# Weights of k and v in a ring of six tiles, those of q in a ring of two, 64 bytes apart

## The chip, the cores and the metric

The kernel runs on one core of one Trainium2 chip. The metric is the device time of one execution in microseconds (us). Where a time comes from the profile, it is from one profiled execution; times inside it count from the start of its span.

## What is computed

A block of attention with a compressive memory, followed by an MLP that mixes tokens, both behind layer norms whose scale and shift come from a condition vector. There are 2048 tokens of 1024 channels, 32 heads of 32, and 4 segments of 512 tokens.

```python
def _A_ref(x, wq, wk, wv, wo, beta):
    q, k, v = (heads of x @ wq, x @ wk, x @ wv)     # 32 heads, 4 segments of 512
    for s in range(4):
        logits = qs @ ks.T * scale + mask           # key <= query is kept
        a_dot = softmax(logits) @ vs
        a_mem = (phi(qs) @ M) / (phi(qs) @ z + 1e-6)
        outs.append(g * a_mem + (1 - g) * a_dot)
        M, z = M + phi(ks).T @ vs, z + sum(phi(ks))
    return o @ wo

x = x + ga * _A_ref(layernorm(x) * (1 + ca) + sa, ...)
h = layernorm(x) * (1 + cb) + sb
x = x + gb * _B_ref(h, ...)     # U = (W2 gelu(W1 LayerNorm(h)^T))^T, F = 3584
```

`sa, ca, ga, sb, cb, gb` are the six parts of `silu(c) @ w_mod`.

## The kernel before

**Stages.** The first stage projects q, k and v and runs the attention; the output projection (`out_proj`) follows, and then the two matrix products of the token MLP (`mix`, line 798), done with seven products in place of eight. Every matrix product of fp32 values is made of three passes: each operand is split into a high part and a low part (`split`, lines 120 and 123: a cast on ACT, a subtraction on DVE), and high times high, high times low and low times high are added up.

**The first stage.** The heads are taken in 8 groups of 4. The work goes in two passes `pr`: the first takes segments 0 and 1 of all groups, the second segments 2 and 3. A pass over one group and one segment is a task `t`, 32 in all: tasks 0 to 15 are the first pass, 16 to 31 the second, and two tasks that follow each other share a group and so its weights. The normalized input of a segment lies in eight "h pages" of 4096 bytes per partition.

A task is projected in four pieces (`project`). Pieces 0 and 1 make k and v, 48 matmuls each (`kv_chunk`, line 193, `nps<-wv,h`: the h page is the stationary operand, the weights stream); piece 2 transposes k (line 363) and makes q, 24 matmuls (`q_chunk`, line 201, `qps<-h,wq`: the weights are stationary, the h page streams). After that, twelve DMAs (`stack`, lines 325 to 327, `sk<-sg`) bring queries and keys of the four heads into the tiles `sk`.

For each head, `maxima` (line 431) computes the scores once for the row maxima. Every second head, the maxima are transposed (line 438, `nmps`), split by ACT and DVE into `nt`, and four small DMAs (line 445, `sk<-nt`) write them into rows 96 and 97 of `sk`. `scores` (lines 466 to 473, `a<-sk`) then computes the scores again with the maxima subtracted; it has to wait for these DMAs. ACT takes the exponential, POOL masks, and `values` (line 495) multiplies by v.

**The weights.** A group has six weight tiles of 4096 bytes per partition: four for k and v together (`wv`, two parts of two tiles) and two for q (`wq`). In the first pass they come as fp32 from the input (`fetch_part`), are split on the chip (`split_part`), and are written to the DRAM tensor `wsp` (`keep_w`, line 174). In the second pass they are read back from `wsp` already split, by one DMA per tile (`load_part`, line 168). All tiles come from one pool, `paw`, with one tag and eight buffers: a ring. A new tile has to wait until the last matmul that reads the buffer's former tile is over. In the order of the tiles (v, v, v, v, q, q for each group) a tile takes the buffer of the tile eight places before it.

**What sets the order.** A scheduler with a timeline of its own orders the instructions of each engine, within the data dependencies and within the places in the program at which the kernel calls for each step. A tile of a ring can be placed only when its buffer is free on that timeline. All DMAs are issued from SP, in one queue: also the condition's rows (`rawm`), the output weights (`wor`), the h pages of the second pass (`h<-hT`, line 310), and the results (`oT`).

**Addresses.** Pools opened one after the other lie one behind the other in SBUF. Behind `paw` come the tiles of the projections (`prj`), of the values (`late`) and `sk`. Some pools begin with a small tile that is used for nothing but its size (`pad`, `pad2`, `offset`, each 32 bytes per partition). In this kernel the h pages lie at 1760 + 4096 n, the weight tiles at 97952 + 4096 n.

Of the kernel before, what the change touches and what calls it, by code (L numbers as in the profile page):

```python
# [7 lines left out]
F32 = mybir.dt.float32  # L8
F32R = mybir.dt.float32r
# [9 lines left out]
P = 128  # L19
# [25 lines left out]
def attention_and_mlp(ctx, tc, x, wq, wkv, wo, beta, w1, b1, w2, b2, c, wm_a, wm_b, out):  # L45
# [70 lines left out]
    def split(dst, src, hi_eng, lo_eng):  # L116

        hi, lo = dst[:, 0], dst[:, 1]
        if hi_eng is A:
            A.copy(hi, src)  # L120
        else:
            hi_eng.tensor_copy(hi, src)
        lo_eng.tensor_tensor(lo, src, hi.bitcast(F32), op=ALU.subtract)  # L123
# [20 lines left out]

    paw = tc.tile_pool(name="paw", bufs=1)
    aw = paw.__enter__()
    raw_w = {}

    def fetch_part(g, kind, part):
        r = a.tile([P, D], F32, tag="raw", bufs=3, name=f"raw{kind}{g}_{part}")  # L150
        SY.dma_start(r, (wkv if kind == "v" else wq)[g, :, 1024 * part:1024 * part + 1024])
        return r

    def split_part(g, kind, part, r):

        for i in range(2):
            w = aw.tile([P, 2, 512], F32R, tag="w", bufs=8, name=f"w{kind}0_{g}_{part}_{i}")
            split(w, r[:, 512 * i:512 * i + 512], A, V)
            W[0, g][kind, 2 * part + i] = w

    def load_part(g, pr, kind, part, res):

        if pr == 0:
            split_part(g, kind, part, fetch_part(g, kind, part))
            return
        for i in range(2):
            w = aw.tile([P, 2, 512], F32R, tag="w", bufs=8, name=f"w{kind}{pr}_{g}_{part}_{i}")
            SY.dma_start(w.bitcast(F32), wsp[g, 2 * part + i if kind == "v" else 4 + i])
            res[kind, 2 * part + i] = w

# [5 lines left out]
    def load_w(g, pr):  # L176
        res = W[pr, g] = {}
        for kind, part in (("v", 0), ("v", 1), ("q", 0)):
            load_part(g, pr, kind, part, res)
        if pr == 0:  # L180
            keep_w(g)
# [92 lines left out]
    for ct in range(NK):  # L274
        for part in range(2):
            wm = s1p.tile([P, D], F32, tag="wm", bufs=11, name=f"wm{ct}_{part}")
            last_wm = SY.dma_start(wm, wm_a[part, ct])
            if part == 0:
                V.scalar_tensor_tensor(wm, wm, 1.0, scb, op0=ALU.mult, op1=ALU.mult, accum_out=saca[:, ct, 0:1])
            else:  # L280
                for k in range(NK):
                    T.matmul(scale_ps[:, ct:ct + 1], wm[:, P * k:P * k + P], sc[:, k:k + 1], start=(k == 0),
                             stop=(k == NK - 1), skip_group_check=True)
        if ct < 3:
            load_part(0, 0, *(("v", 0), ("q", 0), ("v", 1))[ct], W[0, 0])
        V.tensor_scalar_add(saca[:, ct, 1:2], scale_ps[:, ct:ct + 1], 1.0)
        h_chunk(s1p, xs[0], 0, ct)
        if ct:
            first_chunk(ct - 1)
    first_chunk(NK - 1)  # L290
    left.__exit__(None, None, None)
    prj = tc.tile_pool(name="prj", bufs=1, reuse_waits="tile")
    pj = prj.__enter__()
    late = tc.tile_pool(name="late", bufs=1, reuse_waits="tile")
    b = late.__enter__()
    skp = [tc.tile_pool(name=f"sk{i}", bufs=1, reuse_waits="tile") for i in range(2)]
# [309 lines left out]
    for g in range(2, NG):  # L606
        n = 8 * g - 13
        plan(n, lambda g=g: W.__setitem__((0, g), {}))
        for kind, part, n0, n1 in (("v", 0, 0, 1), ("v", 1, 1, 3), ("q", 0, 2, 4)):
            later(n + n0, lambda g=g, kind=kind, part=part: fetch_part(g, kind, part),  # L610
                  n + n1, lambda r, g=g, kind=kind, part=part: split_part(g, kind, part, r), "A")
        plan(n + 4, lambda g=g: keep_w(g))
    for j in range(32):
        n = ML0 + MLS * j
        later(n, lambda j=j: mod_fetch(j), n + 2, lambda r, j=j: mod_late(j, r), "V")
    plan(WO0 - 3, lambda: spread(gaw, 0))
    for i in range(8):
        n = WO0 + WOS * i
        later(n, lambda i=i: wo_fetch(i), n + 2, lambda r, i=i: wo_split(i, r), "G")

    for n in range(-LEADS, 4 * NI + VL):
# [15 lines left out]
        if 4 * NI - 5 <= m < 4 * NI + 3:  # L637
            i = m - 4 * NI + 5
# [4 lines left out]
            with behind(n, engines):  # L643
                f()
    right.__exit__(None, None, None)
    for q in skp + [late, prj, paw]:
        q.__exit__(None, None, None)


# [6 lines left out]
    w = cw_pool.__enter__()  # L656
# [344 lines left out]
```

## Time and profile before

| | us |
|---|---|
| median of 3 runs | 2305.62 |
| lowest and highest | 2304.03, 2310.8 |
| the profiled execution | 2305.58 |
| its span | 2303.9 |

The engines are PE (TensorE matmul), PEld (its weight loads, which overlap PE), DVE (VectorE), ACT (ScalarE), POOL (GpSimd) and SP (SyncE, which here only issues DMAs; SPq is its queue). A name like `qps<-h,wq` is the tile written and the tiles read, L201 a line of the kernel. Matmuls are pipelined: one takes about 0.39 us from its start to its end, and the next starts before that, so the pace of a row of matmuls is the distance of their starts. The clock is the share of its full clock that TensorE was granted.

### The profile page before, as it was taken

The numbers are of one execution on the slowest core, as the hardware profiler recorded it, in microseconds if no ns is written. First come the engines' busy times: TensorE is split into PE (matmuls) and PEld (weight loads), VectorE is DVE, ScalarE is ACT, GpSimd is POOL, SyncE is SP. The second block draws the span as 40 slices with busy tenths as digits, with TensorE's granted clock in tenths as the row PEclk, the third lists the DMA queues.
The fourth block names the chain that finished last, engine by engine and source line by source line (L and its number), as shares of the span: only waits on it lengthen the run. The fifth ranks groups of instructions, "written<-read, shape, count | busy, mean of one in ns | idle before, by whom it ended". The sixth has DMA issues, their size and how long they took to land.

```text
span 2303.9 us, 38456 instructions
## 1 busy us (share of the span) xinstructions
PE 2232.7 (97%) x13866; PEld 1918.9 (83%) x13866; DVE 1703.9 (74%) x3814; ACT 1105.6 (48%) x2018; POOL 727.9 (32%) x835
## 2 busy tenths in 40 slices
PE   8989999998999999999999999999999999999999
PEld 7879888898998889977787888888887888888877
DVE  5666666775777777657988665688889787878787
ACT  5477766755656656654324333543334242424232
POOL 3165655655666767653001000023333000000000
PEclk9989999999999999989999999999999999999999
DMA  6656555677566566663466664556557441414133
GB/s 256 199 164 183 173 162 162 195 247 225 156 199 206 166 189 187 202 212 112 137 205 213 249 237 181 202 222 239 206 201 263 171 151 55 151 55 142 55 119 146
DMA packets 172593, 414.67 MB, mean 180 GB/s; under 512 B 17236, under 2 KB 71540, under 8 KB 163444
## 3 DMA queue, kind: packets, MB, share of 16 engines
q1 hardware_dynamic: 172404, 412.22, 54.7%
q8 instruction: 110, 1.80, 0.3%
q14 instruction: 79, 0.65, 0.1%
HBM read 236.23 MB, written 125.06 MB: 157 GB/s over the span
## 4 chain that ended last, share of the span: by engine, by line
PE 81%; DVE 9%; DMA 5%; ACT 2%; issue 1%; POOL 1%; SPq 0%; DVEq 0%; ACTq 0%
PE mx L798 41%; PE nps L193 14%; PE qps L201 7%; PE po L706 6%; PE pv L495 3%; DMA wr<-in_w_dram 1%; PE a L466 1%; PE sx L431 1%; DVE ac L805 1%; PE sz L431 1%; DVE bU L123 1%; PE rd L403 1%; DVE sp L123 1%; DMA sk<-nt 1%; PE a L469 1%
## 5 line engine op out<-in xcount | busy, mean ns | idle before, releaser
L798 PE MATMUL mx<-bU,sp 128*128 128x512 f32 x2352 | 537.0, 390 | 4.7 <-DVE ac L805 2.0
L798 PEld LDWEIGHTS mx<-bU,sp 128*128 128x128 f32 x2352 | 440.4, 188 | 100.8 <-DVE sp L123 2.7
L193 PE MATMUL nps<-wv,h 128*128 128x256 f32 x3072 | 438.2, 284 | 0.7 <-DVE sg L123 0.5
L798 PE MATMUL mx<-bA,sp 128*128 128x512 f32 x1764 | 432.0, 390 | 2.5 <-DVE sp L123 2.2
L120 ACT CAST sp<-wr 128x384 fp32r<-128x384 f32 (+2 forms) x408 | 217.1, 545 | 449.9 <-PE mx L798 379.6
L481 POOL TENSOR_TENSOR ph<-p,ph 128x640 f16<-128x640 f32 x256 | 379.6, 1504 | 159.0 <-ACT ph L479 153.5
L193 PEld LDWEIGHTS nps<-wv,h 128*128 128x128 f32 x3072 | 403.8, 190 | 6.8 <-DVE sg L123 0.7
L798 PEld LDWEIGHTS mx<-bA,sp 128*128 128x128 f32 x1764 | 330.5, 188 | 73.5 <-DVE sp L123 2.9
L123 DVE TENSOR_TENSOR sp<-wr,sp 128x384 fp32r<-128x384 f32 (+2 forms) x408 | 256.8, 641 | 29.4 <-ACT sp L120 29.2
L805 DVE TENSOR_TENSOR ac<-mx,ac 128x512 f32<-128x512 f32 x280 | 189.3, 685 | 91.2 <-PE mx L798 90.5
L201 PE MATMUL qps<-h,wq 128*128 128x512 f32 x768 | 200.7, 406 | 1.4 <-DVE r L356 1.4
L432 DVE CUSTOM_DVE_ANT_0 sx<-sx,mask 128x128 f32<-128x128 f32 (+1 forms) x256 | 109.5, 428 | 113.6 <-PE sx L431 111.9
L706 PE MATMUL po<-wo,ots 128*128 128x512 f32 x768 | 184.8, 400 | 5.3 <-DVE x L709 3.1
L479 ACT CAST ph<-p 128x1280 f16<-128x1280 f32 x128 | 160.8, 1257 | 41.1 <-POOL p L477 40.3
L706 PEld LDWEIGHTS po<-wo,ots 128*128 128x128 f32 x768 | 148.3, 194 | 38.0 <-issue 3.9
L201 PEld LDWEIGHTS qps<-h,wq 128*128 128x128 f32 x768 | 144.4, 194 | 30.2 <-DVE r L356 1.2
L798 PE MATMUL mx<-bB,sp 128*128 128x512 f32 x588 | 164.3, 389 | 0.0
L477 POOL TENSOR_SCALAR_AFFINE_SELECT p<-p 128x256 f32<-128x256 f32 x256 | 120.5, 480 | 129.2 <-ACT p L470 63.4
L495 PE MATMUL pv<-vp,ph 128*128 128x97 bf16 (+1 forms) x2560 | 146.6, 204 | 5.5 <-DVE mv L134 2.7
L495 PEld LDWEIGHTS <-ph 128*128 128x128 f16 x2560 | 117.5, 100 | 29.4 <-issue 12.1
L805 DVE TENSOR_TENSOR cc<-mx,cc 128x512 f32<-128x512 f32 x140 | 94.6, 683 | 49.9 <-PE mx L798 45.4
L798 PEld LDWEIGHTS mx<-bB,sp 128*128 128x128 f32 x588 | 110.4, 188 | 23.4 <-ACT bB L120 0.6
(173 smaller groups left out, 3206.0 us busy)
## 6 DMA issues: line engine op xcount, KB each, us to landing
sk<-sg SPq DMA_DIRECT2D x384, 128.0 KB
wr<-in_w_dram SPq DMA_DIRECT2D x28, 1024.0 KB
wr<-in_w_dram SPq DMA_DIRECT2D x32, 768.0 KB
bstu<-ucd SPq DMA_DIRECT2D x28, 768.0 KB
wsp<-wv SPq DMA_DIRECT2D x32, 512.0 KB
rawm<-in_wm_b_dram SPq DMA_DIRECT2D x32, 512.0 KB
wv<-wsp SPq DMA_DIRECT2D x32, 512.0 KB
pcd<-cc SPq DMA_DIRECT2D x14, 1024.0 KB
```

The source lines that it names most:

```text
L120: A.copy(hi, src)
L123: lo_eng.tensor_tensor(lo, src, hi.bitcast(F32), op=ALU.subtract)
L193: T.matmul(ps[:, aa], h[:, j, 128 * tt:128 * tt + 128], wt[:, i, o:o + 256], start=(n == 0), stop=(n >= 6 * NK - 2), skip_group_check=True)
L201: T.matmul(ps, wt[:, i, o:o + 128], h[:, j], start=(k + n == 0), stop=(3 * k + n == 3 * NK - 1))
L432: marks[4 * t + h - LEADS, "V"] = V.tensor_tensor_reduce(o, o, mask[:, 384 - 128 * i:], 1.0, -3.0e38, op0=ALU.add, op1=ALU.max, accum_out= ...
L477: G.affine_select(w, w, pattern=[[0, 2], [1, 128]], compare_op=ALU.is_ge, fill=0.0, base=0, channel_multiplier=-1)
L479: marks[n, "A"] = A.copy(ph[:, 0], p32)
L481: marks[n, "G"] = G.tensor_tensor(ph[:, 1, c], p32[:, c], ph[:, 0, c], op=ALU.subtract)
L495: T.matmul(pv[:, i, 0:w], ph[:, part, o:o + 128], d["vp"][:, j, h, 0:w], start=(n == 0), stop=(n == 19), skip_group_check=True)
L706: T.matmul(ps, os_[:, i, P * ct:P * ct + P], wop[ct, nh][:, j], start=(n == 0), stop=(n == 3 * NK - 1))
L798: T.matmul(ps, ops[q][:, i, P * k:P * k + P], b[:, j], start=(m == 0 and first), stop=(m == 3 * nk - 1), skip_group_check=True)
L805: V.tensor_tensor(d, ps, d, op=ALU.add)
```

## The change

The one ring of eight tiles becomes two: six buffers for the tiles of k and v in the pool `paw`, and two buffers for the tiles of q in a pool of their own, `paq`, opened behind it. The new pool begins with an unused tile of 64 bytes per partition, `pad3`, so the q tiles start 64 bytes behind the end of the others, and every pool that is opened later on this side during the first stage lies 64 bytes further on. The number of weight tiles, eight, is the same.

```diff
     paw = tc.tile_pool(name="paw", bufs=1)
     aw = paw.__enter__()
+    paq = tc.tile_pool(name="paq", bufs=1)
+    awq = paq.__enter__()
+    awq.tile([P, 16], F32, name="pad3")
+
+    def weight_tile(kind, name):
+        pool, n = (aw, 6) if kind == "v" else (awq, 2)
+        return pool.tile([P, 2, 512], F32R, tag="w" + kind, bufs=n, name=name)
+
     raw_w = {}
...
     def split_part(g, kind, part, r):
 
         for i in range(2):
-            w = aw.tile([P, 2, 512], F32R, tag="w", bufs=8, name=f"w{kind}0_{g}_{part}_{i}")
+            w = weight_tile(kind, f"w{kind}0_{g}_{part}_{i}")
             split(w, r[:, 512 * i:512 * i + 512], A, V)
             W[0, g][kind, 2 * part + i] = w
...
             split_part(g, kind, part, fetch_part(g, kind, part))
             return
         for i in range(2):
-            w = aw.tile([P, 2, 512], F32R, tag="w", bufs=8, name=f"w{kind}{pr}_{g}_{part}_{i}")
+            w = weight_tile(kind, f"w{kind}{pr}_{g}_{part}_{i}")
             SY.dma_start(w.bitcast(F32), wsp[g, 2 * part + i if kind == "v" else 4 + i])
             res[kind, 2 * part + i] = w
...
-    for q in skp + [late, prj, paw]:
+    for q in skp + [late, prj, paq, paw]:
         q.__exit__(None, None, None)
```

## The prediction

> **What bounds the kernel now.** I read the page's busy shares and its chain first, then stretches of time, then who waited for whom.
>
> ```profile
> PE 2232.7 (97%) x13866; PEld 1918.9 (83%) x13866; DVE 1703.9 (74%) x3814; ACT 1105.6 (48%) x2018; POOL 727.9 (32%) x835
> PE 81%; DVE 9%; DMA 5%; ACT 2%; issue 1%; POOL 1%; SPq 0%; DVEq 0%; ACTq 0%
> ...
> 0.00:485.00 485.00, 452.40 (x3710) 410.33 (x3711) 325.67 (x950) 320.39 (x604) 256.42 (x328) 0.96 0.62 187
> 485.00:1040.00 555.00, 536.23 (x4635) 486.46 (x4633) 381.35 (x1182) 335.50 (x595) 356.33 (x430) 0.97 0.66 199
> 1040.00:2303.90 1263.90, 1244.05 (x5528) 1022.09 (x5526) 996.85 (x1684) 449.73 (x820) 115.15 (x79) 1.00 0.48 169
> ```
>
> TensorE bounds it: 97% busy, 81% of the chain that ended last. The three lower lines are stretches of time (length, then busy time of PE, PEld, DVE, ACT, POOL, then granted clock, DMA share, GB/s). The weights that change place are used in the first two; TensorE is idle there for 485 - 452.4 = 32.6 us and 555 - 536.2 = 18.8 us. A change of buffers can give back only such idle time, the loss of clock that goes with it, or matmul pace. Who does TensorE wait for?
>
> ```profile
> PE a L466 <- DMA sk<-nt: 8.2, 4, 2.8
> PE kps L363 <- DVE r L356: 8.2, 5, 4.1
> PE nps L193 <- ACT wv L120: 0.2, 1, 0.2
> ```
>
> These are total us, times, longest, over the whole run. For weights TensorE waits once, 0.2 us; no line names wq. The ring of eight costs TensorE nothing now, so freeing its tiles earlier cannot pay by itself.
>
> **The change, part by part.**
>
> *Waits on the rings.* With one ring of eight and six tiles per group, the first two v tiles of a group take over the q tiles of two groups before, the other v tiles the first v tiles of the group before, and the q tiles its last v tiles. With six and two, the later v tiles wait for the same tiles as now, the first two v tiles may come earlier, and each q tile waits for the q tile of the group just before, so it is released by a q matmul, not by the last kv matmul. One group boundary of the second pass, tasks 17 to 18:
>
> ```profile
> 582.07 0.64 PE L193 MATMUL nps<-wv,h 128*128 128x256 f32 x4
> 584.61 4.36 PE L201 MATMUL qps<-h,wq 128*128 128x512 f32 x18
> 590.83 0.63 PE L201 MATMUL qps<-h,wq 128*128 128x512 f32 x2
> 613.06 3.62 PE L201 MATMUL qps<-h,wq 128*128 128x512 f32 x15
> 616.98 1.78 PE L201 MATMUL qps<-h,wq 128*128 128x512 f32 x7
> ```
>
> Now the loads may start when the last kv matmul is over, at 582.7. After the change the second one must wait for the last q matmul, at 591.5, which leaves 613.1 - 591.5 = 21.6 us to the next q matmul. Each load is 0.524 MB; at the stretch's 199 GB/s that is 2.6 us (my estimate), 5.3 us for both. The wait is covered four times over. In the first pass ACT and DVE write the tiles:
>
> ```profile
> L120 ACT CAST wq<-rawq x16: 603/623/648, 18.9 to 475.4; 128x512 fp32r<-128x512 f32 x16
> L123 DVE TENSOR_TENSOR wq<-rawq,wq x16: 680/1494/1904, 19.5 to 477.3; 128x512 fp32r<-128x512 f32 x16
> ```
>
> Two tiles cost 2 x (0.62 + 1.49) = 4.2 us there, in a gap of the same kind. Queued behind a waiting split are ACT's copies of scores and projections; behind a waiting load, SP's transfers of keys, queries and maxima. If the cover went, each of the seven group boundaries of a pass would cost TensorE up to the load, some 5 us. Taken: 0, bounds 0 and 2 us.
>
> *Order.* The scheduler frees tiles at other moments, so it orders some instructions anew. In the built program each engine holds the same instructions. The order is the same up to the end of task 12's scores and task 14's queries, that is to about 485 us, and again after task 31's last transposes; between, 1,644 of 16,170 TensorE entries stand elsewhere, 340 of DVE's 3,774, 176 of ACT's 2,018, 110 of SP's 1,238 and 75 of POOL's 838. So the first stretch cannot gain from order, nor the third. In the second, TensorE alternates between kinds of matmul 2,213 times instead of 2,207; the 18-row above gives a bound for one alternation (pace below): (4.36 - 0.39) - 17 x 0.2267 = 0.12 us. Six make +0.7 us.
>
> *Placement.* In the built program the q tiles start 64 bytes further on (122,592 against 118,432 + 4,096) and so do the pools after them. Modulo 2,048 bytes a q tile then lies as the h pages do; now it lies 64 bytes off. Operands that lie alike, and q as it is:
>
> ```profile
> L193 PE MATMUL nps<-wv,h 128*128 128x256 f32 x3072 | 438.2, 284 | 0.7 <-DVE sg L123 0.5 <-ACT wv L120 0.2
> 1498.61 1.98 PE L798 MATMUL mx<-bA,sp 128*128 128x512 f32 x8
> 1500.42 0.84 PE L798 MATMUL mx<-bB,sp 128*128 128x512 f32 x3
> L798 PE MATMUL mx<-bB,sp 128*128 128x512 f32 x588 | 164.3, 389 | 0.0
> L201 PE MATMUL qps<-h,wq 128*128 128x512 f32 x768 | 200.7, 406 | 1.4 <-DVE r L356 1.4
> ```
>
> Take one matmul's 0.39 us from a row and divide by the rest: mx with bB (alike modulo 2,048) goes at (0.84 - 0.39)/2 = 0.225 us, with bA (256 bytes off) at (1.98 - 0.39)/7 = 0.227 us; q, in the boundary's last two rows, at (3.62 - 0.39)/14 = 0.2307 to (1.78 - 0.39)/6 = 0.2317 us. (A kv matmul, in that boundary's first row: (0.64 - 0.28)/3 = 0.12 us.) So lying alike does no harm, and q is 4 to 5 ns over the best pace: 768 x 4.5 ns = 3.5 us at most, if it is the place and not the neighbours of q in this stage. Bounds 0 and -3.5; I take -1.5, nearer to nothing, since bA is as fast without lying alike. The Trainium skill (TensorE: Matmul & The Clock Gate, what happens when you issue a matmul, LDWEIGHTS step) gives TensorE two independent read ports, one for the moving operand and one for weights, so placement would matter nothing. By that rule this term is 0.
>
> *Stalls.* The rest is which short transfers come late in the second stretch.
>
> ```profile
> 523.32 0.56 PE L466 MATMUL a<-sk 98*128 98x512 f32 x1 [1.85 <-DMA sk<-nt]
> 544.69 0.50 PE L466 MATMUL a<-sk 98*128 98x512 f32 x1 [1.32 <-DMA sk<-nt]
> 556.39 0.47 PE L466 MATMUL a<-sk 98*128 98x512 f32 x1 [1.81 <-ACT p L474]
> 702.54 0.47 PE L466 MATMUL a<-sk 98*128 98x512 f32 x1 [2.21 <-DMA sk<-nt]
> 786.41 0.77 PE L466 MATMUL a<-sk 98*128 98x512 f32 x1 [2.83 <-DMA sk<-nt]
> ...
> 523.60:527.00 3.40, 3.40 (x15) 3.12 (x14) 1.50 (x6) 1.75 (x3) 1.59 (x3) 0.50 0.96 349
> 557.70:564.50 6.80, 6.10 (x28) 5.34 (x28) 4.35 (x14) 3.52 (x6) 5.43 (x5) 0.50 0.38 122
> 786.40:789.80 3.40, 3.39 (x26) 2.91 (x27) 0.59 (x2) 2.52 (x4) 0.61 (x1) 0.50 0.00 0
> ```
>
> Three of these are followed by a stretch at half clock, 3.4 or 6.8 us long, which costs half its length again: 1.7 or 3.4 us. The Trainium skill (same page, HAM oscillation) says to avoid TensorE gaps over about 3.4 us; these rows show half clock after gaps of 1.8 to 2.8 us, so the rows disagree with that limit. By it a new 2 us stall would cost its 2 us alone.
>
> The stall at 702.5 (task 19, heads 2 and 3) comes from this queue:
>
> ```profile
> 691.09 1.60 SPq L168 DMA_DIRECT2D wv<-wsp  x1
> 692.73 0.43 SPq L520 DMA_DIRECT2D rawm<-in_wm_b_dram  x1
> 693.21 0.44 SPq L578 DMA_DIRECT2D wor<-in_wo_dram  x1
> 693.75 0.41 SPq L520 DMA_DIRECT2D rawm<-in_wm_b_dram  x1
> 694.26 0.38 SPq L168 DMA_DIRECT2D wv<-wsp  x1
> 694.73 0.39 SPq L168 DMA_DIRECT2D wq<-wsp  x1
> 696.93 2.64 SPq L445 DMA_DIRECT2D sk<-nt  x4
> ```
>
> Six large loads go ahead of the four small ones, and only 39 matmuls stand between the transpose of the maxima and the waiting score matmul. After the change task 19 has 65 there, 24 of them of q (24 x 0.23 = 5.5 us): that stall goes. Task 25 comes to exactly the old case, 39 matmuls of the same kinds instead of 62 and six large loads ahead: +2.2. In task 22 it is 31 instead of 42 (13 kv matmuls fewer, bounded by 13 x 0.12): +1.5 on 2.83. In tasks 13 and 14 TensorE has less between as well (116 to 75, 159 to 119), but two v loads leave the crowd ahead of those transfers. Sum: -2.2 + 2.2 + 1.5 = +1.5, with one or two half-clock stretches either way, -5 to +5.
>
> **Sum.** 0 + 0.7 - 1.5 + 1.5 = +0.7 us on the profiled execution's 2305.58 (span 2303.9 and 1.7 around it), which lies 0.04 under the median of 2305.62: **2306.3 us**. With the bounds of the terms (-9 to +9) the forecast's own range is 2297 to 2315.
>
> **Rivals.** *Slower: the small transfers of tasks 13 and 14 stay where they are and TensorE arrives earlier.* Against 523.3, 41 matmuls fewer stand ahead, 22 of them of q: 22 x 0.231 = 5.1 us more stall. Against 544.7 there are 40 fewer, 23 of kv (23 x 0.12 = 2.8). With a half-clock stretch more for each (2 x 1.7): +11.3 on the forecast, 2317.6. For it: 96% DMA share and 349 GB/s in the row of 523.6, a full queue. Against: the first two v loads of the second pass go out before task 12's transfers and take 1 MB, about 3 us at that rate, out of the crowd. It decides if those small transfers land less than some 4 us earlier after task 13's queries than now.
>
> *Faster: the emptier queue removes the stalls at 523, 545 and 556* and their half clock: 1.85 + 1.32 + 1.81 + 1.7 + 3.4 = 10.1, that is 2296.2. For it: the same two loads. Against: TensorE's orders above take away as much slack as the queue gains.
>
> *Placement is worth more, or less, than the q rows show.* All 3.5 us give 2304; sk and the projections' tiles move by 64 bytes too, and no row prices that. It stays within the range.
>
> *The change does nothing:* 2305.6, if order and queue drift cancel; it falls within the forecast's class.
>
> **Numbers.** 0.3% is 6.9 us, about what a measurement of this kernel can tell from no change. Forecast and the two cases near it, within 6.9 us: 0.50. The slower rival, or the forecast's own upper end: 0.30. The faster one, or its lower end: 0.20. To leave out no more than 2 in 10 the range must reach past both rivals: 2294 to 2321. The likeliest case's own range is 2297 to 2315.
>
> **What would show it.** Right: the q loads in the second pass go out after the last q matmul of the group before, and no wait names wq; the first 485 us keep their length to 2 us; q's pace falls to about 0.227 us; the stall at task 19 is gone and one at task 25 is there. Wrong: a wait of TensorE for wq, by which the cover was not there; kv or q pace worse by over 5 ns, by which placement costs; stalls at L466 in tasks 13 to 15 that add to over 10 us, the slower rival; or a change in the third stretch, where only addresses before it differ.

## The result, and the profile after

| | before | after |
|---|---|---|
| median, us | 2306.98 (10 runs on the same chip) | 2313.77 (10 runs) |
| lowest and highest | 2303.33, 2310.8 | 2305.68, 2319.48 |
| ratio to before, 95% interval | | 1.003 (1.0016 to 1.0043) |
| the profiled execution | 2305.58 | 2319.48 (span 2317.8) |

The change costs 6.8 us, 0.3%. The profiled execution of after is the slowest of its ten, 5.7 us over the median; that of before lies 1.4 us under its median. So no length of after below is read alone: the same order of instructions was profiled twice more, in `rings_no_gap` and `rings_again` below, at 2305.98 and 2308.0 us, each the fastest execution of its kernel. The order of before was profiled twice more as well, in `one_ring_gap` and `one_ring_shifted`.

The busy line of after's page, then the prediction's three stretches (length, busy PE, PEld, DVE, ACT, POOL, granted clock, DMA share, GB/s):

```profile
PE 2237.2 (97%) x13866; PEld 1923.5 (83%) x13866; DVE 1701.2 (73%) x3814; ACT 1107.6 (48%) x2018; POOL 722.1 (31%) x835
```

```profile
0.00:485.00 485.00, 452.00 (x3680) 410.96 (x3681) 324.84 (x938) 319.00 (x601) 254.11 (x324) 0.96 0.60 186
485.00:1040.00 555.00, 532.34 (x4621) 482.16 (x4619) 371.85 (x1181) 334.25 (x590) 346.59 (x425) 0.98 0.63 194
1040.00:2303.90 1263.90, 1244.17 (x5531) 1023.87 (x5532) 999.39 (x1690) 454.38 (x828) 121.39 (x88) 0.99 0.48 170
```

TensorE still bounds the kernel. Its busy time in the first and third stretch is as before (452.40 and 1244.05); in the second it fell from 536.23 to 532.34, which is 3.9 us more idle time in 555 us. Stretches at fixed times hold different work, so the next view cuts at marks of the program: the first q matmul of tasks 14, 16, 18, 24 and 31, and the first matmul of the output projection of the ninth of its 16 token tiles. Before, then after:

```profile
487.60:549.21 61.61, 58.16 (x488) 52.42 (x488) 37.02 (x117) 30.89 (x58) 28.79 (x37) 0.97 0.88 300
549.21:613.06 63.85, 61.30 (x538) 56.07 (x537) 41.93 (x132) 37.91 (x68) 38.50 (x45) 0.95 0.60 167
613.06:790.28 177.22, 171.38 (x1526) 157.47 (x1526) 128.66 (x389) 110.42 (x198) 122.21 (x144) 0.99 0.64 188
790.28:991.59 201.31, 198.55 (x1787) 182.94 (x1786) 140.45 (x442) 128.02 (x227) 135.45 (x167) 1.00 0.61 178
991.59:1057.04 65.45, 57.66 (x404) 46.70 (x403) 42.35 (x122) 36.26 (x60) 42.21 (x50) 0.86 0.60 198
sum 569.44, PE 547.05 PEld 495.60 DVE 390.40 ACT 343.49 POOL 367.17; mean PE 109.41 PEld 99.12 DVE 78.08 ACT 68.70 POOL 73.43
```

```profile
490.83:554.85 64.02, 59.80 (x514) 54.16 (x513) 37.79 (x123) 34.68 (x63) 31.77 (x42) 0.95 0.89 289
554.85:612.20 57.35, 57.21 (x527) 52.73 (x525) 38.82 (x127) 36.08 (x66) 35.18 (x43) 1.00 0.57 167
612.20:792.35 180.15, 171.37 (x1506) 156.37 (x1504) 126.72 (x385) 109.65 (x196) 116.87 (x142) 0.99 0.62 185
792.35:1002.07 209.72, 204.59 (x1809) 187.39 (x1809) 140.45 (x445) 130.27 (x229) 138.15 (x168) 0.98 0.57 171
1002.07:1069.44 67.37, 56.51 (x387) 44.37 (x384) 43.88 (x125) 34.97 (x58) 39.65 (x49) 0.89 0.60 200
sum 578.61, PE 549.48 PEld 495.03 DVE 387.67 ACT 345.65 POOL 361.62; mean PE 109.90 PEld 99.01 DVE 77.53 ACT 69.13 POOL 72.32
```

In both the five rows hold 4,743 matmuls, though some have crossed from one row to the next. Tasks 14 to 18 take 4.1 us less than before (121.37 against 125.46), all later rows 13.3 us more. TensorE's idle time over the five is 569.44 - 547.05 = 22.4 us before, 578.61 - 549.48 = 29.1 us after.

Who it waits for there (total, times, longest, from 485 to 1070 us), before and after:

```profile
PE a L466 <- DMA sk<-nt: 8.2, 4, 2.8
PE pv L495 <- DVE mv L134: 2.7, 1, 2.7
PE sz L431 <- DVE mx L432: 2.5, 2, 2.3
PE a L466 <- ACT p L474: 1.8, 1, 1.8
```

```profile
PE a L474 <- DMA sk<-nt: 9.2, 6, 4.0
PE pv L503 <- DVE red L510: 3.7, 4, 2.1
PE sx L439 <- DVE mx L440: 2.9, 2, 2.7
PE po L714 <- DMA wo<-wos: 2.2, 1, 2.2
PE po L714 <- ACT ots L120: 1.7, 1, 1.7
PE pv L503 <- POOL v L348: 1.5, 1, 1.5
```

The small transfers `sk<-nt`, the only waits that the prediction counted, rose by 1.0 us in this execution. That is no more than scatter: they come to 6.8 to 9.6 us in the three profiles of before's order and to 7.1 to 9.2 us in the three of after's. The others are waits for vector results, copies and output weights: the three others of before went or shrank to 0.6 us or less, and the five others of after were not there before or were shorter. Four of these five come back in both other profiles of after's order; the one for `mx` does not (0.8 and 0.4 us there). The three that before never shows at this size, in `rings_no_gap`:

```profile
PE po L713 <- DMA wo<-wos: 3.8, 1, 3.8
PE pv L502 <- DVE red L509: 3.7, 4, 2.1
PE pv L502 <- POOL v L347: 1.5, 1, 1.5
```

No wait names wq.

### The profile page after: what moved, and what is told of

Read it like the earlier page. It is cut to its first block, busy times and chain, and to the rows that moved or that the text cites. A ratio compares the mean times of both kernels' runs of the same rounds, so it can differ in the third digit from the quotient of the medians.

```text
span 2317.8 us, 38439 instructions
## 1 busy us (share of the span) xinstructions
PE 2237.2 (97%) x13866; PEld 1923.5 (83%) x13866; DVE 1701.2 (73%) x3814; ACT 1107.6 (48%) x2018; POOL 722.1 (31%) x835
## 4 chain that ended last, share of the span: by engine, by line
PE 75%; DMA 10%; DVE 9%; ACT 2%; issue 2%; POOL 1%; SPq 1%; DVEq 0%; ACTq 0%; POOLq 0%
PE mx L806 37%; PE nps L201 12%; PE qps L209 8%; PE po L714 5%; PE pv L503 3%; DMA xb<-x1d 2%; DMA x1e<-xb 2%; DMA sk<-nt 1%; PE a L474 1%; PE sx L439 1%; DVE bU L123 1%; PE sz L439 1%; DMA x<-in_x_dram 1%; PE rd L411 1%; PE a L477 1%
## 5 line engine op out<-in xcount | busy, mean ns | idle before, releaser
L489 POOL TENSOR_TENSOR ph<-p,ph 128x640 f16<-128x640 f32 x256 | 374.1, 1482 | 156.1 <-ACT ph L487 150.3
L209 PE MATMUL qps<-h,wq 128*128 128x512 f32 x768 | 205.5, 414 | 1.5 <-DVE r L364 1.5
L209 PEld LDWEIGHTS qps<-h,wq 128*128 128x128 f32 x768 | 149.7, 201 | 31.6 <-issue 1.6
L503 PEld LDWEIGHTS <-ph 128*128 128x128 f16 x2560 | 116.7, 100 | 31.4 <-issue 11.4
```

Source lines behind the costliest of these rows:

```text
L209: T.matmul(ps, wt[:, i, o:o + 128], h[:, j], start=(k + n == 0), stop=(3 * k + n == 3 * NK - 1))
L489: marks[n, "G"] = G.tensor_tensor(ph[:, 1, c], p32[:, c], ph[:, 0, c], op=ALU.subtract)
L503: T.matmul(pv[:, i, 0:w], ph[:, part, o:o + 128], d["vp"][:, j, h, 0:w], start=(n == 0), stop=(n == 19), skip_group_check=True)
```

## The experiments

In each table the ratio is to runs of the kernel before on the same chip.

**Is it the order or the place?** The change does two things after 485 us: it re-sorts instructions, and it moves tiles by 64 bytes. Four kernels separate them. `rings_no_gap` keeps the two rings, and so after's order on every engine, but drops the gap, so that the q tiles and the later pools lie as before:

```diff
     awq = paq.__enter__()
-    awq.tile([P, 16], F32, name="pad3")
```

> The two rings without the 64 bytes between them: every engine's order of instructions is that of the changed kernel, every tile but q's lies where it lay before, and q is again 64 bytes off the h pages (modulo 2,048). If the new order from about 485 us on costs the 6.8 us: 2312 to 2317, that is 5 to 10 above the kernel before, with the stalls at the score matmuls of tasks 13 and 25 there. If the placement costs it: within 3 us of the kernel before. The pace of a row of q matmuls should go back from 0.227 to about 0.230 us, which is worth 2 us.

`one_ring_gap` is the kernel before, in its order, with only the unused 64 bytes behind the one ring, so that the later pools lie as after:

```diff
     aw = paw.__enter__()
+    paq = tc.tile_pool(name="paq", bufs=1)
+    awq = paq.__enter__()
+    awq.tile([P, 16], F32, name="pad3")
```

> One ring of eight as before, with 64 unused bytes behind it: every engine's order is that of the kernel before, the weight tiles lie where they lay, and all pools behind them (projections, values, sk) lie 64 bytes further on, as in the changed kernel. If order costs the 6.8 us: within 3 us of the kernel before, 2304 to 2310. If the shift of those pools costs it: 2311 to 2316. q stays at 0.230 us.

`one_ring_shifted` puts the 64 bytes ahead of the ring, so that all eight weight tiles lie as the h pages do modulo 2,048 bytes; the order is that of before:

```diff
     aw = paw.__enter__()
+    aw.tile([P, 16], F32, name="pad3")
```

> One ring of eight as before, but all eight tiles 64 bytes further on, and the pools behind them too: the order of the kernel before, and both q and the kv weights now lie as the h pages do modulo 2,048. If lying alike is what brings q to 0.227 us, q goes to 0.227 here too (2 us gained) and the kv matmuls go from a mean of 119.7 ns to some 117 or less (up to 6 us gained): 2299 to 2305. If the pace of q came from something else in the changed kernel: no change of pace, 2304 to 2310. If kv is worse when alike: slower, over 2310.

`rings_again` is after unedited. It ran late, beside the last experiment below.

> The changed kernel once more, unedited, on the same chip as the kernel with the earlier load, so that the two stand against the same runs of the kernel before. Both theories: 1.002 to 1.0045, TensorE idle 28 to 30 us from task 14's queries to po8_0, and the wait for wo<-wos of 2 to 4 us there again.

| kernel | order | median us | ratio, 95% interval | five rows: length, PE busy, idle |
|---|---|---|---|---|
| before | before | | | 569.4, 547.1, 22.4 |
| one_ring_gap | before | 2306.29 | 1.0001 (0.999 to 1.0013) | 569.2, 546.5, 22.7 |
| one_ring_shifted | before | 2306.16 | 1.0005 (0.9993 to 1.0016) | 571.0, 549.8, 21.2 |
| after | after | 2313.77 | 1.003 (1.0016 to 1.0043) | 578.6, 549.5, 29.1 |
| rings_no_gap | after | 2312.49 | 1.0033 (1.002 to 1.0046) | 574.7, 546.3, 28.5 |
| rings_again | after | 2316.54 | 1.0037 (1.0019 to 1.0055) | 574.8, 548.2, 26.6 |

All kernels in the order of before are within 0.16% of it, wherever the tiles lie; all in the order of after lose 0.3%, with the gap or without. The cost is that of two rings and the order that comes with them. The idle time parts the kernels the same way: 21 to 23 us against 27 to 29. Row by row, over three profiles each:

| TensorE idle, us | order of before | order of after |
|---|---|---|
| tasks 14 to 16 | 3.5 to 4.0 | 3.7 to 4.2 |
| tasks 16 to 18 | 1.5 to 3.2 | 0.1 |
| tasks 18 to 24 | 4.2 to 5.8 | 6.6 to 8.8 |
| tasks 24 to 31 | 2.5 to 3.1 | 4.4 to 5.1 |
| task 31 to the output projection | 7.3 to 8.8 | 10.9 to 13.1 |

So the new order gains in the second row and loses in the last three, most of all in the last.

Of the expectations, that of `one_ring_shifted` missed: q became faster as it says, but the kv matmuls became slower and the time stayed where it was (see the last section). For `rings_again`, 28 to 30 us idle and a wait of 2 to 4 us for wo were expected, and 26.6 and 1.4 came.

**How much of it is clock?** Most runs are on record with the mean clock that TensorE was granted. It averages 0.983 in each of three sets of runs of before and in `one_ring_gap`, and 0.982, 0.9825 and 0.981 in after, `rings_no_gap` and `rings_again`. Time multiplied by clock is an estimate of the time at full clock: 2267 us in the three sets of before and in `one_ring_gap`, 2271 to 2273 us in the three of after's order. By it 4 to 5.5 us of the loss would be there at full clock too, and the other 2 to 5 us go with the lower clock. No run parts the two: where the prediction shows stretches at half clock, they follow waits of TensorE, so the lower clock can itself come from longer waits.

**Do the early v loads crowd the queue?** In `rings_v_behind_q` the first two v loads of each group in the second pass stay behind the q loads of the group before, as the one ring had them (the lines that note the last load are left out here):

```diff
...
-            load_part(g, pr, kind, part, res)
+            with ExitStack() as s:
+                if pr and (kind, part) == ("v", 0):
+                    s.enter_context(tc.issue_after(last_load["q"].ins))
+                load_part(g, pr, kind, part, res)
```

> The two rings and the 64 bytes, but in the second pass the loads of a group's first two v tiles are queued on SP behind the loads of q of the group before, as the one ring forced them to be; q's tiles still wait for the q matmuls of the group before. TensorE's order is a third one. If early v loads crowding the queue ahead of the small transfers of the maxima are what costs the time: 2304 to 2309, with the waits for those transfers back to some 8 us or less. If any new order costs something by the stalls it happens to hold: anywhere from 2304 to 2318, and no less waiting than in the changed kernel (some 11 us for the small transfers).

Measured: 2313.22 us, 1.0033 (1.0017 to 1.0048), idle 29.8 us, 9.8 us of it for the small transfers. Task 13's wait, the first line, is short, but others are long:

```profile
526.33 0.47 PE L478 MATMUL a<-sk 98*128 98x512 f32 x1 [1.17 <-DMA sk<-nt]
788.83 0.77 PE L478 MATMUL a<-sk 98*128 98x512 f32 x1 [3.66 <-DMA sk<-nt]
1024.74 0.80 PE L443 MATMUL sz<-sk 96*128 96x512 f32 x1 [3.35 <-DVE mx L444]
```

The edit sorted TensorE's instructions into a third order, neither before's nor after's. So it shows that late v loads alone do not give the time back, not what they cost by themselves.

**Do the weight loads ahead of the small transfers cost it?** In `rings_nt_first` and `one_ring_nt_first` a group's loads in the second pass are issued behind the small transfers of the maxima just traced, with two rings and with one (the lines that note the last small transfer are left out):

```diff
...
-                with tc.issue_after(last_sk[0, 3].ins):
+                with tc.issue_after((last_nt[0] if its[t][0] else last_sk[0, 3]).ins):
                     load_w(its[t][1], its[t][0])
```

> The changed kernel, with the loads of a second-pass group's weights queued on SP behind the small transfers of the maxima of heads 2 and 3 of the task two before the group's first. Those transfers then have no weight load right ahead of them, and TensorE's order is sorted anew. If the changed kernel lost its 7 us by weight loads ahead of the small transfers: 2304 to 2308, with TensorE's waits for them at no more than 5 us (10.9 in the changed kernel), the one of task 13 (4.0 and 3.7 us in two executions of that order) under 2. If the loss is spread over whatever waits a new order holds: still 2308 to 2317, the wait of task 13 smaller and others in its place.

> The same queueing with the one ring of eight of the kernel before. If the small transfers are what costs: faster than the kernel before by the part of its 8.2 us and their half clock that goes, 2297 to 2303. If a new order mostly trades waits: 2304 to 2316.

Measured: 2320.65 us, 1.0062 (1.0045 to 1.008), idle 35.0, and 2312.04 us, 1.0028 (1.0014 to 1.0043), idle 28.9. Task 13's wait is down to 0.5 us with two rings, but the waits for small transfers still come to 7.2 us, and to 9.5 us with one ring. So moving the loads does not remove these waits. With two rings these stand out, the second of them for a weight tile:

```profile
785.59 0.77 PE L475 MATMUL a<-sk 98*128 98x512 f32 x1 [3.97 <-DMA sk<-nt]
827.07 1.12 PE L201 MATMUL nps<-wv,h 128*128 128x256 f32 x6 [1.65 <-DMA wv<-wsp]
973.28 0.63 PE L519 MATMUL ops<-ident,am 128*128 128x128 f32 x4 [3.61 <-POOL p L486]
```

**Are two q buffers too few?** `rings_4_4` gives four to each kind:

```diff
-        pool, n = (aw, 6) if kind == "v" else (awq, 2)
+        pool, n = (aw, 4) if kind == "v" else (awq, 4)
```

> Two rings of four, 64 bytes apart: eight tiles as ever, but now q's tiles are free a whole group early, and the first v tiles wait for the first v tiles of the group before. If it is the late release of q's tiles that costs: 2304 to 2308. If any new order costs: 2308 to 2318; a price of the v tiles' later release would show as a wait of the kv matmuls for wv. q should run at 0.227 us in rows.

Measured: 2323.34 us, 1.0072 (1.005 to 1.0094), idle 30.9. Task 13's wait is as long as after's:

```profile
525.05 0.77 PE L474 MATMUL a<-sk 98*128 98x512 f32 x1 [4.21 <-DMA sk<-nt]
```

No wait of TensorE names wv or wq. Spare q buffers do not help; whether v's ring of four costs by itself was not separated.

**What does any new order cost?** `mx3` leaves the weights as before and gives a small tile of maxima a third buffer, an edit that has nothing to do with the rings:

```diff
-            d["mx"] = b.tile([P, 2, 4], F32, tag="mx", bufs=2, name=f"mx{t}_{h}")
+            d["mx"] = b.tile([P, 2, 4], F32, tag="mx", bufs=3, name=f"mx{t}_{h}")
```

> One ring of eight as before, and one change that has nothing to do with weights: the tile of the row maxima has three buffers of 32 bytes instead of two. No instruction is added and one constraint is loosened; the scheduler sorts the order anew (4,932 of 16,170 TensorE entries elsewhere, more than by the rings). If the order of the kernel before is simply a good one of many, this one costs as well: 2308 to 2320. If only orders with late q loads cost: 2302 to 2308.

Measured: 2310.07 us, 1.0011 (0.9997 to 1.0024), idle 21.9; 4,932 of TensorE's entries moved. Unclear, at most 0.24%. So a new order can be nearly free, but of the six orders tried none beat that of before, and five are slower by 0.28 to 0.72%.

**Is a single wait behind it?** At the end of the stage the eighth load of output weights stands behind all twelve `sk<-sg` transfers of task 31 in after, where before all eight went in a row. `rings_wo_first` moves it ahead of the first nine, and leaves every other instruction of every engine at its place:

```diff
-            for h in range(3):
+            for h in range(3 if t < NI - 1 else 0):
                 stack(t, h)
...
+            if m == 4 * NI - 2:
+                with tc.issue_after(last_wo.ins):
+                    for h in range(3):
+                        stack(NI - 1, h)
```

> The changed kernel, with the last page of the output weights (the eighth wo<-wos load) issued ahead of the first nine sk<-sg transfers of task 31 instead of behind all twelve; every other instruction keeps its place on every engine. In the changed kernel that load goes out at 1023.2 us, and the first output projection waits for it 2.2 us (3.8 us without the gap); before, all eight loads go out in one row and nothing waits. Theory that the loss is a sum of separate waits that the new order makes, this one among them: the wait goes, TensorE's idle time from task 14's queries to po8_0 falls from 29 to 25 to 27 us, and the time falls by 2 to 4 us, to a ratio of 1.000 to 1.0025 against the kernel before. Rival, that the last task's chain of maxima bounds the end of the stage (before: 2.3 us for the maxima and 2.7 for a vector at the same place): the wait moves to the maxima, pv or po's results, the idle time stays, and the ratio stays near 1.003.

Measured: 2310.73 us, 1.0027 (1.0013 to 1.004), idle 26.0, against 1.0037 (1.0019 to 1.0055) for `rings_again` on the same chip. The waiting matmul of `rings_again`, then, in `rings_wo_first`, the place of the load, the same matmuls without the wait, and a wait behind them:

```profile
1017.72 0.96 PE L714 MATMUL po<-wo,ots 128*128 128x512 f32 x3 [1.43 <-DMA wo<-wos]
```

```profile
1004.38 0.34 SPq L649 DMA_DIRECT2D wo<-wos  x1
1015.50 1.83 PE L718 MATMUL po<-wo,ots 128*128 128x512 f32 x7
1023.12 0.66 PE L518 MATMUL ops<-ident,am 128*128 128x128 f32 x4 [3.76 <-DVE nt L449]
```

The wait for the weights went, and the one for the split maxima, 4 to 5 us further on, is 3.8 us long, where `rings_again` has 1.1 us. The last of the five rows is 69.2 us long, not shorter than after's 67.4 or `rings_again`'s 66.3. That is what the rival expected: the last task's chain of maxima sets the end of the stage. The idle time tells nothing here: 26.0 us lies where the other theory put it, but `rings_again`, without the edit, has 26.6. The intervals overlap, so a small gain is neither shown nor excluded; but the kernel stays at least 0.13% over before, so this wait is not the whole cause.

## Why the prediction was right or wrong

Forecast 2306.3 us in a range of 2294 to 2321; measured 2313.77, 0.3% slower than before, on the border between the cases "within 0.3%" (0.5) and "slower" (0.3). The time lies within the range, and even within the likeliest case's own 2297 to 2315, but the sum put +0.7 us where +6.8 came. That it fits is owed to the width of the bounds, not to the mechanism. (As stated, the bounds of the terms add up to -7.8 and +7.7, not to -9 and +9; the measured change is near their upper end.)

*Waits on the rings, taken as 0: the traces agree.* TensorE waits for no q tile in after, though its q loads go out later: the first 38.1 us behind task 14's first q matmul, against 32.7 before.

*First stretch the same to 2 us: not decidable from one execution.* Task 14's queries begin 3.2 us later in after, but 1.3 us earlier in `rings_no_gap` and 2.3 us earlier in `rings_again`, which have the same order. That is the scatter of executions.

*Order, taken as +0.7 us: not visible.* By the lines of the kernel, TensorE changes from one kind of matmul to another 2,012 times in before's trace and 2,013 times in after's. The pace of 0.2267 us in that sum lies between the two mx rows shown and stands in neither. Alternations are not what the new order costs.

*Placement, taken as -1.5 us: the pace is right, the time not visible.* A matmul of q (least, median, most ns) before, after, and in the two kernels that put its place and its order apart, `rings_no_gap` and `one_ring_shifted`:

```profile
L201 PE MATMUL qps<-h,wq x768: 387/394/776, 28.1 to 996.9; 128*128 128x512 f32 x192
```

```profile
L209 PE MATMUL qps<-h,wq x768: 387/389/775, 28.1 to 1008.1; 128*128 128x512 f32 x192
```

```profile
L208 PE MATMUL qps<-h,wq x768: 387/394/767, 28.1 to 996.7; 128*128 128x512 f32 x192
```

```profile
L202 PE MATMUL qps<-h,wq x768: 387/389/775, 28.0 to 1003.4; 128*128 128x512 f32 x192
```

The median is 389 ns where q lies as the h pages do and 394 where it is 64 bytes off, whatever the order. So place does act on the pace, against what the prediction drew from the two independent read ports in the Trainium skill (TensorE: Matmul & The Clock Gate, what happens when you issue a matmul). In time it cannot be told from nothing: with and without the gap the ratios are 1.003 and 1.0033, and the busy time of all q matmuls did not fall (200.7 us before, 205.5 after, 202.3 in `rings_no_gap`). The prediction's "lying alike does no harm" is wrong for kv: the kv row that it shows has its weights 64 bytes off the h pages, and where kv was made to lie alike, it became slower (last section). In after the kv tiles stay where they were.

*Stalls, taken as +1.5 us with bounds of -5 and +5: the step that failed.* It priced only the waits for small transfers, and their sum did not change (8.2 us before, 9.2 in after, 7.1 and 8.5 in the two other profiles of its order). One by one it was right about task 19 (gone) and task 25 (new: 1.88 us, and 0.97 and 2.52 in `rings_no_gap` and `rings_again`, against the 2.2 forecast), wrong about task 22 (1.60, 1.04 and 2.01 us, where 2.83 + 1.5 was forecast). It took every other wait of the re-sorted stretch as unchanged, without giving a reason. Those waits (vector sums, copies, values, output weights) make up most of the 4 to 7 us of idle time that the three profiles of this order have over before. Since place shows nothing in time and no wait names wq, the change of 6.8 us is put down to this term, part of it through the clock; no run measures it alone.

*The two rivals that priced tasks 13 and 14 were each half right.* The slower one needs task 13's transfers to stay where they are while TensorE comes earlier. (In task 14 the traces hold 167 matmuls in that place before and 121 after, not 159 and 119.) Task 13's wait, and the queue ahead of its transfers, after and then before:

```profile
517.08 0.39 SPq L528 DMA_DIRECT2D rawm<-in_wm_b_dram  x1
517.56 0.39 SPq L176 DMA_DIRECT2D wv<-wsp  x1
518.04 2.63 SPq L453 DMA_DIRECT2D sk<-nt  x4
523.16 0.76 PE L474 MATMUL a<-sk 98*128 98x512 f32 x1 [3.98 <-DMA sk<-nt]
```

```profile
516.66 0.39 SPq L520 DMA_DIRECT2D rawm<-in_wm_b_dram  x1
517.14 0.38 SPq L168 DMA_DIRECT2D wv<-wsp  x1
517.61 2.63 SPq L445 DMA_DIRECT2D sk<-nt  x4
```

The same loads stand ahead: the two v loads that left early had not been in this crowd. The wait grew by 3.98 - 1.85 = 2.1 us, of the 5.1 that the rival gave it. The faster rival's part came true beside it: the waits of 1.32 and 1.81 us in task 14 are gone, and tasks 16 to 18 are 63.85 - 57.35 = 6.5 us shorter. Together tasks 14 to 18 take 121 us in the three profiles of after's order and 124 to 125.5 us in those of before's, a gain of 2.5 to 4 us. The loss lies behind them, in tasks 18 to 31 and the end of the stage, where the prediction had looked at three waits only.

*What stays open.* Two rings and their order were not parted: no kernel has the rings in before's order. That the rings cost nothing by themselves rests on the absence of waits of TensorE for their tiles. There is a way that this does not show: a load that waits for its buffer holds up SP's queue, and the small transfers stand in the same queue. From 485 to 1060 us, SP waits for kv and q matmuls ahead of weight loads for 11.4 to 13.7 us in the three profiles of before's order and for 17.4 to 22.6 us in those of after's. But `mx3`, with one ring, has 22.4 us too and loses at most 0.24%. So this is not shown to cost anything, and not excluded. The loss is spread over many waits of 1 to 4 us; the one that was taken out alone gave place to another.

## What to carry to other kernels

Where a scheduler orders the program, changing a buffer count changes the order far beyond that buffer: build it, see how much moves, and give the moved stretch a cost of its own, with bounds from other re-sorted versions (in six here from no clear change to 0.7%, never a gain), instead of a sum over the waits that one can name. To tell order from place, build one kernel with the new place in the old order and one with the old place in the new order. A wait at the end of a stage that several chains reach together can be worth little: here, when the one named last was removed, the next stood there.

## What the hardware showed that was not expected

**The same 64 bytes help one kind of matmul and hurt another.** With the weights lying as the h pages do, q (weights stationary) is 5 ns shorter; kv (h page stationary) is longer. The medians of kv before and in `one_ring_shifted`:

```profile
L193 PE MATMUL nps<-wv,h x3072: 276/278/562, 27.1 to 989.0; 128*128 128x256 f32 x192
```

```profile
L194 PE MATMUL nps<-wv,h x3072: 274/283/562, 27.0 to 995.5; 128*128 128x256 f32 x192
```

A row of 44 kv matmuls early in the first pass takes 5.17 us before and 5.43 in `one_ring_shifted`, 6 ns more for each. Over 3,072 that would be some 15 to 18 us. The busy time of all kv matmuls rose by less, to 446.1 us from 438.2 before and 440.4 in `one_ring_gap`, and the time of the kernel by at most 0.16%, 3.7 us. Part of the reason is on record: the twelve runs of `one_ring_shifted` were granted a mean clock of 0.985, those of before 0.983. Time multiplied by clock, the estimate used above, is 2273 us against 2267, so some 5 us were lost and most of them came back by the clock. Why the clock was higher is open. So is whether the distance to the h pages counts or the address itself, since the h pages lie at the same place in all runs.

**Half clock after short gaps, and not after each.** Of after, the granted clock of two stretches, and the gap at the start of each:

```profile
84.80:88.20 3.40, 3.29 (x14) 3.20 (x15) 3.00 (x7) 3.40 (x8) 0.00 (x0) 0.50 1.05 263
866.00:870.00 4.00, 3.31 (x30) 3.15 (x30) 2.45 (x10) 2.48 (x4) 2.98 (x3) 1.00 0.69 158
```

```profile
84.91 1.22 PE L201 MATMUL nps<-wv,h 128*128 128x256 f32 x4 [0.88 <-ACT wv L120]
866.69 0.47 PE L474 MATMUL a<-sk 98*128 98x512 f32 x1 [0.99 <-DMA sk<-nt]
```

A gap of 0.88 us goes with 3.4 us at half clock, one of 0.99 us with none. So the length of one gap does not decide it. The work around it differs: the 3.4 us ahead of the first row (81.4 to 84.8 us) held 1.83 us of matmuls, with two shorter gaps ahead of this one; the two stretches of 3.4 us that the second gap straddles (863.0 to 866.4 and 866.4 to 869.8 us) held 2.71 and 3.11 us. Two cases are not a rule, but a price of half clock per stall, as the prediction has it, does not hold for each stall.
